# A chain of attention and two feed-forward blocks: stage 1 of batches 2 and 3 moved to slots 36 to 50, and splits tied to their slot

## The chip, the cores and the metric

The kernel runs on one core of a Trainium2 chip. The metric is the device time of one execution in microseconds; the time before is the median of three runs. A core has a matrix engine (PE, with its weight loads shown as PEld), a vector engine (DVE), an activation engine (ACT), a general engine (POOL) and a queue engine (SP) that only issues transfers here. Each engine works through its own list of instructions in order and waits where an input or a buffer isn't ready. Matrix products go to PSUM, which this kernel uses as eight banks.

## The reference

```python
def sm_attn(qq, kk, vv):                      # scale = 1/sqrt(64)
    s = scale * np.matmul(qq, kk.transpose(0, 1, 3, 2))
    s = s - np.max(s, axis=-1, keepdims=True)
    a = np.exp(s)
    a = a / (np.sum(a, axis=-1, keepdims=True) + 1e-09)
    return np.matmul(a, vv)
p_packed = sm_attn(p, k, v)                   # 32 rows per head: "stage 1", a pack
out = sm_attn(q, p_packed, p_packed)          # "stage 2", a spread
x = out.transpose(0, 2, 1, 3).reshape(4608, 512)
h = x @ w_in                                  # 512 -> 2048
x2 = (h / (1 + np.exp(-h))) @ w_out           # 2048 -> 512
y = ((x2 @ w1) * (x2 @ w2)) @ w3 @ wo2        # 512 -> 1024 -> 1024 -> 512
```

There are 8 batches, 8 heads, 576 positions, 64 values per head. All is float32. The weights arrive as 64-bit words and are turned into float32 on the chip ("decoding").

## The kernel before

**Numbers.** A float32 factor is split into a high part, in the type fp32r, and the rest as a low part; a product is three matmuls (`mm3`, lines 97 to 100): high × high, low × high, high × low. So nearly every factor has a split: `split_hi` (line 82) copies on ACT, `split_lo` (line 91) subtracts on DVE or, where the engine is given as G, on POOL.

**Slots.** The first feed-forward block is a list of 256 items (b, f, m): batch, half of its positions (288), and one of 16 slices of 128 of the 2048 inner columns. An item is a slot of the main loop. Batches 0 and 1 come first, with slices 0 to 7 in slots 0 to 31 and 8 to 15 in slots 32 to 63; batch 2 takes slots 64 to 95, and so on. A slot issues six matmuls into `ps_h`; sg (ACT, a tanh) and gg (DVE) from it, the split of gg into gh and gl (ACT and POOL), and twelve matmuls into `ps_x` for the item three slots back. The `ps_h` factors are a2, the result of stage 2 for this batch, and mq, a slice of the attention-packed w_in. `fetch` loads mq slices one by one through `mr` and splits them (DVE and POOL); it holds eight of them.

**What feeds the slots.** The product of softmax weights, packed values and w_in is regrouped: stage 1 (`Pack`) makes 32 packed rows per head; `PackIn` multiplies them, placed in the block matrix mbd, by w_in and stores the result in DRAM (`m_d`); stage 2 (`Spread`) turns q and the packed rows into softmax weights a2. A batch has two units of Pack and two of Spread (four heads each). For batch 2 the first slot that needs a2 is 64; `fetch` begins to load its `m_d` at slot 57. PackIn has 16 products: a w_in tile wz from DRAM, split into wi (three buffers), one mm3 into the bank `ps_m`, a copy ms (two buffers) and two stores.

**Order.** Each stream of side work is a Python generator. `over(lo, hi, units)` and `pack_in(lo, hi, batches)` spread a list's steps evenly over slots lo to hi (`due`), and the main loop advances the streams after each slot's own instructions. `chain` runs the units in a row: the steps of one unit also carry hooks, which load and split the next unit's inputs (`load`, `load_v`, `turn0`, `turn1`, `prepare`, `split_v0`). Packs and spreads share single buffers for the splits (x, v, e, pb), and packs, spreads and PackIn's products take turns on the two PSUM banks of the pool `ps_f`. A program written out by hand (`START`) orders the decoding of w_in and w_out (the "fill") through slot 34, beside the attention of batches 0 and 1.

This emission order is a priority, not the order on the engines. A planner with a timing model goes through the program: whenever an engine is free in the model, it takes the ready instruction that was emitted first. So later work may be pulled forward where an engine is idle, and late work falls behind its slot. `tc.issue_after(i)` forbids it for what stands in its block: on i's engine nothing of it goes ahead of i. `hold("sg", "gg")` does this with the last sg (on ACT) and the last gg (on DVE). Loads emitted in slots 0 to 15 are kept behind the last weight load; later ones are free (the lines `if i == KM` in the main loop and `move`).

Of the kernel before, what the change touches and what calls it, by code (L numbers as in the profile page):

```python
# [23 lines left out]
def attention_swiglu_chain(  # L24
# [54 lines left out]
    V, A, T, G, DMA = nc.vector, nc.scalar, nc.tensor, nc.gpsimd, nc.sync  # L79

    def act_copy(dst, src, mul=1.0):
        A.activation(out=dst, in_=src, func=ACTF.Copy, scale=mul)  # L82

    def split_hi(hi, src, on_vector=False):
        if on_vector:
            V.tensor_copy(out=hi, in_=src)  # L86
        else:
            act_copy(hi, src)

    def split_lo(lo, src, hi, eng=None):  # L90
        (eng or V).tensor_tensor(out=lo, in0=src, in1=hi.bitcast(F32), op=ALU.subtract)  # L91

    def split(hi, lo, src, on_vector=False, eng=None):
        split_hi(hi, src, on_vector)
        split_lo(lo, src, hi, eng)
# [8 lines left out]
    def hold(*names):  # L104

        stack = ExitStack()
        for x in names:
            stack.enter_context(tc.issue_after(behind[x]))
        return stack

    def move(out, in_, eng=DMA):

        out, in_ = (x.bitcast(F32) if x.dtype == F32R else x for x in (out, in_))
        with tc.issue_after(behind[eng]) if eng in behind else ExitStack():
            return eng.dma_start(out=out, in_=in_)  # L115
# [113 lines left out]
    def q_blocks(i, plain):  # L229
        return blocks(f"sbd{i}", [128, 2, 2, 128], plain)  # L230
# [4 lines left out]
    def small(n, name):  # L235
        return at.tile([128, n], F32, tag=f"{name}{n}", name=name, bufs=2)
# [7 lines left out]
    def work(shape, name):  # L244
        return at.tile(shape, F32, tag="work", name=name, bufs=3)

    def fill_blocks(dst, src, plain):

        quads = [slice(32 * h, 32 * h + 32) for h in range(4)]
        for r in quads:  # L250
            (act_copy if plain else V.tensor_copy)(dst[r, 0, :, r], src[r])  # L251
        for r in () if plain else quads:
            V.tensor_tensor(
                out=dst[r, 1, :, r], in0=src[r], in1=dst[r, 0, :, r].bitcast(F32), op=ALU.subtract
            )
# [44 lines left out]
    class Rows:  # L300
# [25 lines left out]
        def turn(self, f):  # L326

            if f not in self.halves or self.lane.plain:
                return
            if f == self.halves[0]:  # L330
                self.xp = self.lane.parts([128, 2, S], "x")
            x = [t[:, :, f * HS:(f + 1) * HS] for t in self.xp]
            split(*x, self.rows[f])
            self.x[f] = [[t[:, e] for t in x] for e in range(2)]

        def turn0(self):
# [18 lines left out]
            pass  # L355

        prepare = load_v = split_v0 = tail = nothing

    class Pack(Rows):

# [4 lines left out]
        N = 4  # L365
        PARTS = [(128, slice(0, 3)), (96, slice(3, 5))]
        HOOKS = {0: ["load_v"], 1: ["turn0"], 2: ["turn1", "prepare"], 3: ["split_v0"]}
# [14 lines left out]
        def prepare(self):  # L382
            if not self.lane.plain:
                self.pb = self.lane.parts([128, 2, 128], "pb")
                split(*self.pb, self.p)

        v_in_pieces = False

# [15 lines left out]
        def split_v(self, f):  # L404
            if self.lane.plain:
                return
            if f == 0:
                self.vp = self.lane.parts([128, 5, 4, 64], "v")
            r, cs = self.PARTS[f]
            hi, lo, src = (x[0:r, cs] for x in (*self.vp, self.v))  # L410
            split_hi(hi, src)
            split_lo(lo, src, hi, G)

        def split_v0(self):
            self.vp = [self.v]
# [2 lines left out]
        def steps(self):  # L418
            b, hg = self.b, self.hg
            sc = self.scores(self.pb)  # L420
            mx, nb, sm, rs = small(2, "mx"), small(1, "nb"), small(2, "sm"), small(1, "rs")
            for f in range(2):
                V.tensor_reduce(out=mx[:, f:f + 1], in_=sc[f][:, 0:HS], axis=AX.X, op=ALU.max)
            V.tensor_tensor(out=nb, in0=mx[:, 0:1], in1=mx[:, 1:2], op=ALU.max)
            V.tensor_scalar(out=nb, in0=nb, scalar1=-scale, scalar2=None, op0=ALU.mult)
            e1 = work([128, S], "e1")
            for f in range(2):
                A.activation(
                    out=e1[:, f * HS:(f + 1) * HS], in_=sc[f][:, 0:HS], func=ACTF.Exp, scale=scale,
                    bias=nb, accum_out=sm[:, f:f + 1],  # L430
                )
            self.split_v(1)
            yield
            ep = self.lane.parts([128, 5, 128], "e")
            pts = []
            o = 0
            for r, cs in self.PARTS:
                pt = self.lane.bank("ps_t")
                n = cs.stop - cs.start
                for j in range(n):  # L440
                    T.transpose(pt[0:r, 128 * j:128 * j + 128], e1[:, o:o + r], ident)
                    o += r
                pts.append(pt[0:r, 0:128 * n].rearrange("p (j n) -> p j n", j=n))
            for et, (r, cs) in zip(pts, self.PARTS):
                split_hi(ep[0][0:r, cs], et)
                if not self.lane.plain:
                    split_lo(ep[1][0:r, cs], et, ep[0][0:r, cs])
            V.tensor_tensor(out=rs, in0=sm[:, 0:1], in1=sm[:, 1:2], op=ALU.add)
            V.tensor_scalar(out=rs, in0=rs, scalar1=EPS, scalar2=None, op0=ALU.add)
            V.reciprocal(out=rs, in_=rs)  # L450
            yield
            po = self.lane.bank("ps_o")
            for c in range(5):
                r = 128 if c < 3 else 96
                self.lane.mm(
                    po[:, 0:256].rearrange("p (h d) -> p h d", h=4),
                    [x[0:r, c] for x in ep], [(x[c] if self.v_in_pieces else x[:, c])[0:r] for x in self.vp], c == 0, c == 4,
                )
                if c == 2:
                    yield  # L460
            self.pk = at.tile([128, 2, 64], F32, tag="pk", name="pk", bufs=2)
            for h in range(4):
                r = slice(32 * h, 32 * h + 32)
                A.activation(
                    out=self.pk[r], in_=po[r, 64 * h:64 * h + 64].unsqueeze(1).to_broadcast([32, 2, 64]),
                    func=ACTF.Copy, scale=rs[r],
                )
            pkT = at.tile([128, 2, 32], F32, tag="pkT", name="pkT", bufs=2)
            V.transpose(out=pkT, in_=self.pk[:, 0].rearrange("p (e i) -> p e i", e=2))
            fill_blocks(q_blocks(2 * (b % 2) + hg, self.lane.plain), pkT, self.lane.plain)  # L470
            yield
# [25 lines left out]
    class PackIn:  # L497


        N = 17  # L500
        HOOKS = {}
# [8 lines left out]
        turn0 = turn1 = prepare = load_v = split_v0 = tail = load  # L510

        def load_w(self, i):
            if i < 4 * CD:
                g, c = divmod(i, CD)
                z = at.tile([128, 512], F32, tag="z", name="wz", bufs=NZ)
                move(out=z, in_=wi_d[g, 128 * c:128 * c + 128])
                t = at.tile([128, 2, 512], F32R, tag="wi", name="wi", bufs=WI)
                split_hi(t[:, 0], z)
                split_lo(t[:, 1], z, t[:, 0], G)
                self.w[i] = t  # L520

        def steps(self):
# [27 lines left out]
    class Spread(Rows):  # L550


        N = 4
        HOOKS = {0: ["load_v"], 2: ["turn0"], 3: ["turn1", "prepare", "split_v0"]}
# [179 lines left out]
    def plain(us):  # L734
        for u in us:
            u.lane = lanes[0]
        return us
# [310 lines left out]
    def over(lo, hi, us):  # L1048
        units.extend(us)
        paces["x"].append((lo, hi, sum(u.N for u in us)))  # L1050

    def pack_in(lo, hi, bs):
        ins.append(PackIn(bs))
        paces["y"].append((lo, hi, PackIn.N))

    over(5, 14, plain([Spread(1, 0), Spread(1, 1)]))
    over(26, 38, [Pack(2, 0, 0), Pack(2, 1, 0), Pack(3, 0, 1), Pack(3, 1, 1)])
    pack_in(44, 66, [2, 3])
    over(44, 62, [Spread(2, 0), Spread(2, 1)])
    for b in range(2, B - 2, 2):  # L1060
        n, at0 = b + 2, b * H2
        over(at0 + 8, at0 + 29, [
# [338 lines left out]
```

## Time and profile before

| | |
|---|---|
| median of three runs | 1439.48 us (1436.52 to 1439.56) |
| profiled execution | 1437.96 us, its span 1436.1 us |
| PE busy in the span | 1390.7 us (97%) |
| DVE, ACT, POOL busy | 901.6, 672.2, 605.5 us |
| mean granted TensorE clock | 0.992 |

Slots 0 to 255 run from 44.7 to about 860 us; the second feed-forward block follows. The granted clock is a share of full speed, 2.4 GHz. "Busy" of PE counts a matmul until its end, and matmuls overlap, so the spacing of their starts tells more than their length.

### The profile page before, as it was taken

Reading aid. Unit: us, or ns where it says so; the run is one execution under the profiler, and the core shown is the slowest. Engines: PE = TensorE matmul, PEld = TensorE weight load, DVE = VectorE, ACT = ScalarE, POOL = GpSimd, SP = SyncE. Lnnn points to the kernel's source line nnn. Section 1 sums busy time; section 2 is a strip of 40 time slices with the busy share of each in tenths; the row PEclk is TensorE's granted clock in tenths of the full one; section 3 lists DMA queues with packets and bytes.
Section 4 is the critical chain, followed back from the end, with each engine's and each line's share of the span. In section 5 each row is a group of like instructions: output and inputs, shape, how many; then the busy total and the mean of one; then the engine's idle time right before and its main releaser. Section 6 shows DMA issues by size and latency. Waiting matters only on the chain.

```text
span 1436.1 us, 25890 instructions
## 1 busy us (share of the span) xinstructions
PE 1390.7 (97%) x9548; PEld 1308.4 (91%) x9548; DVE 901.6 (63%) x1687; ACT 672.2 (47%) x1474; POOL 605.5 (42%) x626
## 2 busy tenths in 40 slices
PE   7799899999999999999999999999999999999998
PEld 5578899899999999999998998999999999999998
DVE  5897756558766488666578855635454553645453
ACT  6866556655666555664556544323232231322221
POOL 2778755856779657687567534100000000000000
PEclk9999899999999999999999999999999999999999
DMA  8697544844568343563557667011010110101000
GB/s 319 198 308 253 163 150 142 265 152 146 170 184 249 123 155 121 170 190 116 178 162 252 204 228 298 23 38 46 15 60 1 60 29 31 59 2 60 1 30 30
DMA packets 135967, 193.07 MB, mean 134 GB/s; under 512 B 14496, under 2 KB 92576, under 8 KB 135328
## 3 DMA queue, kind: packets, MB, share of 16 engines
q1 hardware_dynamic: 125344, 178.82, 39.1%
q10 hardware_dynamic: 10496, 12.59, 2.5%
q8 instruction: 75, 1.23, 0.4%
q14 instruction: 52, 0.43, 0.1%
HBM read 132.38 MB, written 58.98 MB: 133 GB/s over the span
## 4 chain that ended last, share of the span: by engine, by line
PE 70%; DVE 9%; DMA 7%; issue 4%; POOL 4%; ACT 4%; SPq 2%; ACTq 0%; DVEq 0%; POOLq 0%
PE ps_ab L1236 24%; PE ps_x L100 6%; PE ps_x L98 6%; PE ps_x L99 6%; PE ps_o L98 5%; PE ps_o L99 5%; PE ps_o L100 5%; PE ps_h L98 3%; PE ps_h L100 3%; PE ps_h L99 3%; SPq L115 2%; DMA mr<-m_d 1%; DMA m_d<-ms 1%; POOL z L189 1%; DVE sbd L251 1%
## 5 line engine op out<-in xcount | busy, mean ns | idle before, releaser
L98 PE MATMUL ps_x<-gh,wo 128*128 128x288 f32 x1024 | 301.9, 298 | 2.7 <-ACT gh L82 1.2
L99 PE MATMUL ps_x<-gh,wo 128*128 128x288 f32 x1024 | 301.0, 296 | 0.0
L100 PE MATMUL ps_x<-gl,wo 128*128 128x288 f32 x1024 | 289.1, 297 | 1.9 <-POOL gl L91 1.6
L91 POOL TENSOR_TENSOR gl<-gg,gh 128x288 fp32r<-128x288 f32 x256 | 227.9, 893 | 101.5 <-ACT gh L82 82.5
L1236 PE MATMUL ps_ab<-xct,w 128*128 128x256 f32 x1728 | 223.0, 284 | 1.7 <-DVE r L1257 1.4
L1236 PEld LDWEIGHTS ps_ab<-xct,w 128*128 128x128 f32 x1728 | 215.6, 190 | 3.0 <-DVE r L1257 1.6
L98 PEld LDWEIGHTS ps_x<-gh,wo 128*128 128x128 f32 x1024 | 193.0, 189 | 6.1 <-DVE xs L883 2.0
L99 PEld LDWEIGHTS ps_x<-gh,wo 128*128 128x128 f32 x1024 | 193.2, 189 | 2.1 <-issue 1.2
L100 PEld LDWEIGHTS ps_x<-gl,wo 128*128 128x128 f32 x1024 | 188.1, 189 | 4.3 <-POOL gl L91 3.6
L82 ACT ACTIVATE gh<-gg 128x288 fp32r<-128x288 f32 x256 | 112.8, 443 | 165.8 <-DVE gg L846 158.2
L91 POOL TENSOR_TENSOR mq<-mr,mq 128x256 fp32r<-128x256 f32 x168 | 136.7, 814 | 109.0 <-DVE mq L86 54.4
L846 DVE SCALAR_TENSOR_TENSOR gg<-sg,ps_h 128x288 f32<-128x288 f32 x256 | 114.6, 448 | 107.3 <-ACT sg L841 55.3
L1236 PE MATMUL ps_ab<-xcb,w 128*128 128x256 f32 x1296 | 177.5, 283 | 0.7 <-ACT w L82 0.4
L98 PE MATMUL ps_h<-a,mq 128*128 128x288 f32 x512 | 155.9, 305 | 18.0 <-DVE gg L846 13.8
L1236 PEld LDWEIGHTS ps_ab<-xcb,w 128*128 128x128 f32 x1296 | 168.1, 189 | 5.6 <-ACT w L82 0.6
L1257 DVE TENSOR_TENSOR r<-p,ps_ab 128x512 f32<-128x512 f32 x72 | 49.2, 683 | 184.3 <-PE ps_ab L1236 184.1
L99 PE MATMUL ps_h<-a,mq 128*128 128x288 f32 x512 | 152.4, 298 | 0.0
L100 PE MATMUL ps_h<-a,mq 128*128 128x288 f32 x512 | 151.9, 297 | 0.0
L841 ACT ACTIVATE sg<-ps_h 128x288 f32<-128x288 f32 x256 | 103.4, 404 | 82.3 <-PE ps_h L100 48.6
L98 PEld LDWEIGHTS ps_h<-a,mq 128*128 128x128 f32 x512 | 96.7, 189 | 25.9 <-DVE gg L846 19.0
L82 ACT ACTIVATE p<-ps_ab 128x512 f32<-128x512 f32 x72 | 43.1, 598 | 146.2 <-PE ps_ab L1236 139.8
L100 PE MATMUL ps_o<-w,abh 128*128 128x512 f32 x280 | 109.5, 391 | 0.0
(172 smaller groups left out, 2645.3 us busy)
## 6 DMA issues: line engine op xcount, KB each, us to landing
mr<-m_d SPq DMA_DIRECT2D x144, 128.0 KB, 2.6
raw<-in_moe_w_dram SPq DMA_DIRECT2D x32, 512.0 KB, 4.4
wz<-wi_d SPq DMA_DIRECT2D x48, 256.0 KB, 3.8
m_d<-ms SPq DMA_DIRECT2D x96, 128.0 KB, 3.0
x_d<-xs SPq DMA_DIRECT2D x20, 576.0 KB, 3.4
raw<-in_moe_w_out_dram SPq DMA_DIRECT2D x22, 512.0 KB, 4.3
out_dram<-ob SPq DMA_DIRECT2D x36, 256.0 KB, 2.0
vr<-in_v_dram SPq DMA_DIRECT2D x14, 640.0 KB, 4.1
```

The source lines that it names most:

```text
L82: A.activation(out=dst, in_=src, func=ACTF.Copy, scale=mul)
L91: (eng or V).tensor_tensor(out=lo, in0=src, in1=hi.bitcast(F32), op=ALU.subtract)
L98: T.matmul(out=dst, lhsT=wh, rhs=xh, start=start, stop=False)
L99: T.matmul(out=dst, lhsT=wl, rhs=xh, start=False, stop=False)
L100: return T.matmul(out=dst, lhsT=wh, rhs=xl, start=False, stop=stop)
L115: return eng.dma_start(out=out, in_=in_)
L189: G.tensor_tensor(out=z, in0=z, in1=word(I32, 0), op=ALU.add)
L251: (act_copy if plain else V.tensor_copy)(dst[r, 0, :, r], src[r])
L841: ins = A.activation(out=sg, in_=ps, func=ACTF.Tanh, scale=0.5)
L846: ins = V.scalar_tensor_tensor(out=gg, in0=sg, scalar=1.0, in1=ps, op0=ALU.add, op1=ALU.mult)
L1236: T.matmul(out=bank[:, x], lhsT=w[:, wp], rhs=xt[:, kt, xp], start=first and (x, kt, n) == (0, 0, 0), stop=last and (x, kt, n) == (1, 1, 2 ...
L1257: V.tensor_tensor(out=dst, in0=p, in1=q, op=op)
```

## The change

Stage 1 of batches 2 and 3 (four packs) is emitted over slots 36 to 50 instead of 26 to 38. A new unit, `Pause`, stands ahead of them at slots 33 to 36: it does nothing itself, but its hooks load and split the first pack's inputs there (before, the hooks of the last Spread of batch 1 did, at slots 10 to 13). Stage 2 of batch 2 goes from 44–62 to 50–63 and PackIn for batches 2 and 3 from 44–66 to 50–70. The splits of q, k, p, v (in all batches that use them) and of PackIn's w_in tiles are emitted inside a `hold`, so that they don't go ahead of the sg and gg of the slot in which they are emitted.

```diff
--- before.py
+++ after.py
@@ -330,7 +330,8 @@
             if f == self.halves[0]:
                 self.xp = self.lane.parts([128, 2, S], "x")
             x = [t[:, :, f * HS:(f + 1) * HS] for t in self.xp]
-            split(*x, self.rows[f])
+            with hold("sg", "gg"):
+                split(*x, self.rows[f])
             self.x[f] = [[t[:, e] for t in x] for e in range(2)]
 
         def turn0(self):
@@ -356,6 +357,17 @@
 
         prepare = load_v = split_v0 = tail = nothing
 
+    class Pause(Rows):
+
+
+        N = 2
+        HOOKS = {0: ["load_v", "turn0", "prepare"], 1: ["turn1", "split_v0"]}
+        load = turn0 = turn1 = Rows.nothing
+
+        def steps(self):
+            yield
+            yield
+
     class Pack(Rows):
 
 
@@ -382,7 +394,8 @@
         def prepare(self):
             if not self.lane.plain:
                 self.pb = self.lane.parts([128, 2, 128], "pb")
-                split(*self.pb, self.p)
+                with hold("sg", "gg"):
+                    split(*self.pb, self.p)
 
         v_in_pieces = False
 
@@ -408,8 +421,9 @@
                 self.vp = self.lane.parts([128, 5, 4, 64], "v")
             r, cs = self.PARTS[f]
             hi, lo, src = (x[0:r, cs] for x in (*self.vp, self.v))
-            split_hi(hi, src)
-            split_lo(lo, src, hi, G)
+            with hold("sg"):
+                split_hi(hi, src)
+                split_lo(lo, src, hi, G)
 
         def split_v0(self):
             self.vp = [self.v]
@@ -515,8 +529,9 @@
                 z = at.tile([128, 512], F32, tag="z", name="wz", bufs=NZ)
                 move(out=z, in_=wi_d[g, 128 * c:128 * c + 128])
                 t = at.tile([128, 2, 512], F32R, tag="wi", name="wi", bufs=WI)
-                split_hi(t[:, 0], z)
-                split_lo(t[:, 1], z, t[:, 0], G)
+                with hold("sg"):
+                    split_hi(t[:, 0], z)
+                    split_lo(t[:, 1], z, t[:, 0], G)
                 self.w[i] = t
 
         def steps(self):
@@ -1054,9 +1069,10 @@
         paces["y"].append((lo, hi, PackIn.N))
 
     over(5, 14, plain([Spread(1, 0), Spread(1, 1)]))
-    over(26, 38, [Pack(2, 0, 0), Pack(2, 1, 0), Pack(3, 0, 1), Pack(3, 1, 1)])
-    pack_in(44, 66, [2, 3])
-    over(44, 62, [Spread(2, 0), Spread(2, 1)])
+    over(33, 36, [Pause()])
+    over(36, 50, [Pack(2, 0, 0), Pack(2, 1, 0), Pack(3, 0, 1), Pack(3, 1, 1)])
+    pack_in(50, 70, [2, 3])
+    over(50, 63, [Spread(2, 0), Spread(2, 1)])
     for b in range(2, B - 2, 2):
         n, at0 = b + 2, b * H2
         over(at0 + 8, at0 + 29, [
```

## Rows read from the trace of the kernel before

**Rows 1.** Busy times by stretch (us, instructions): PE, PEld, DVE, ACT, POOL; clock; DMA

```profile
60.00:137.65 77.65, 70.97 (x451) 61.90 (x451) 65.30 (x98) 52.47 (x112) 64.32 (x60) 1.00 0.93 302
137.65:176.85 39.20, 33.11 (x208) 31.33 (x207) 31.83 (x57) 21.92 (x55) 33.32 (x32) 0.87 0.49 145
...
231.90:268.00 36.10, 36.10 (x249) 34.50 (x247) 26.95 (x52) 21.86 (x47) 23.83 (x24) 1.00 0.73 223
```

**Rows 2.** PE matmuls into ps_h by stretch: us, busy (x count), clock, DMA share, GB/s

```profile
0.00:137.60 137.60, 28.75 (x156) 0.98 0.84 277
...
137.65:176.85 39.20, 10.93 (x60) 0.87 0.49 145
...
189.90:231.90 42.00, 13.58 (x84) 1.00 0.44 139
459.75:471.65 11.90, 4.77 (x30) 1.00 0.70 203
```

**Rows 3.** PE's waits from 137.7 to 176.9: total us, times, longest

```profile
PE ps_h L98 <- DVE gg L846: 4.8, 4, 2.7
```

**Rows 4.** Two stretches with a lower granted clock, columns as in Rows 1

```profile
154.20:157.50 3.30, 3.30 (x15) 3.30 (x15) 2.03 (x5) 3.04 (x9) 3.30 (x4) 0.50 0.92 261
...
167.90:174.60 6.70, 6.05 (x25) 6.05 (x26) 5.00 (x15) 2.21 (x6) 3.11 (x5) 0.50 0.30 98
```

**Rows 5.** PE in order of time: start us, us, line, what it writes and reads

```profile
139.69 0.30 PE L98 MATMUL ps_s<-x,pb 128*128 128x288 f32 x1
...
164.01 0.27 PE L478 MATMUL ps_pk<-ident,pk 128*128 128x128 f32 x1
...
189.86 0.27 PE L478 MATMUL ps_pk<-ident,pk 128*128 128x128 f32 x1
...
231.95 0.27 PE L478 MATMUL ps_pk<-ident,pk 128*128 128x128 f32 x1
...
236.43 0.29 PE L100 MATMUL ps_s<-x,sbd 128*128 128x288 f32 x1
...
254.94 0.29 PE L100 MATMUL ps_s<-x,sbd 128*128 128x288 f32 x1
...
267.16 0.30 PE L98 MATMUL ps_h<-a,mq 128*128 128x288 f32 x1
...
295.23 0.30 PE L98 MATMUL ps_s<-x,pb 128*128 128x288 f32 x1
...
313.17 0.27 PE L478 MATMUL ps_pk<-ident,pk 128*128 128x128 f32 x1
```

**Rows 6.** DVE in order of time, with the idle time before and its releaser

```profile
246.93 0.76 DVE L91 TENSOR_TENSOR a<-sT,a 128x576 fp32r<-128x576 f32 x1
...
259.21 0.29 DVE L86 CAST mq<-mr 128x256 fp32r<-128x256 f32 x1 [1.49 <-DMA mr<-m_d]
...
266.98 0.97 DVE L91 TENSOR_TENSOR a<-sT,a 128x576 fp32r<-128x576 f32 x1 [0.42 <-ACT a L82]
```

**Rows 7.** Two load issues by time, and load sizes: count, KB, us to landing

```profile
73.20 2.62 SPq L115 DMA_DIRECT2D vr<-in_v_dram  x1
106.19 0.59 SPq L115 DMA_DIRECT2D pr<-in_p_dram  x1
...
vr<-in_v_dram SPq DMA_DIRECT2D x14, 640.0 KB, 4.1
...
kq<-in_k_dram SPq DMA_DIRECT2D x26, 288.0 KB, 3.6
```

**Rows 8.** The tile ms, 230 to 290 us: duration ns min/median/max, first and last start

```profile
L115 SPq DMA_DIRECT2D m_d<-ms x32: 445/570/1062, 239.4 to 284.8; - x32
L82 ACT ACTIVATE ms<-ps_m x16: 577/582/602, 238.3 to 283.2; 128x512 f32<-128x512 f32 x16
...
DMA to landing us min/median/max: 2.3/2.9/5.4
```

**Rows 9.** The tile wi, 140 to 235 us, columns as in Rows 8

```profile
L91 POOL TENSOR_TENSOR wi<-wz,wi x3: 1274/1343/1353, 153.9 to 160.0; 128x512 fp32r<-128x512 f32 x3
```

## Prediction

> **What bounds the kernel now.** The profiled execution took 1437.96 us: its span of 1436.1 and 1.9 around it. The median of the runs shown is 1439.48, 1.5 more; I work on the former and add 1.5 at the end.
>
> First the stretches [rows 1]. The reader should see three kinds. In 60 to 137.65 us the DMA engines are 0.93 busy at 302 GB/s, and PE idles for 6.7 of 77.65 us. In 137.65 to 176.85 PE is busy for 33.1 of 39.2 us at a granted clock of 0.87, while DVE (31.8) and POOL (33.3) are nearly as full. In 231.9 to 268 PE is busy throughout.
>
> Then the slots. Each issues six ps_h matmuls. 156 have started by 137.60 us, so slot 26 starts at about 137.7; the next 60, slots 26 to 35, take up to 176.85. A slot with nothing beside it takes 11.9 / 5 = 2.38 us [rows 2], so these ten should need 23.8 us and took 39.2. In the 15.4 us between lie the first pack's PE work and the scores of the second. A pack costs PE about 4.3 us (the 42.0 us between two pack ends hold 84 ps_h [rows 2], so 14 slots or 33.3 us, and two packs); the second's scores are 12 matmuls at 2.38 / 18 = 0.13 us, 1.6. That leaves 9.5 us of real loss. PE waited 4.8 us there for gg on DVE [rows 3], and in two stretches ran 3.3 and 6.05 busy us at a granted clock of 0.50 [rows 4], which is the 1.2 of its two levels (1.2 and 2.4 GHz); half of that is 4.7. The two account for the 9.5.
>
> Last the chain that ends at slot 64, the first use of a2, batch 2's second-stage result. A pack is a serial chain (scores, exp, transposes, values, its closing transpose ps_pk) over two PSUM banks. The closing transposes of packs 1, 2 and 4 stand at 164.01, 189.86 and 231.95 [rows 5]: 24.3 us after the first scores at 139.69 for the pack in the fill, 25.9 for the second, 21.05 each for the last two. So four packs that are emitted over slots 26 to 38 really ran until slot 53; the emission window is not what paces them. The last a2 split ended at 266.98 + 0.97 = 267.95 [rows 6], and slot 64 starts at 267.16 [rows 5]. There is no slack.
>
> **The change, part by part.**
>
> *Packs 26–38 become 36–50, prepared by the Pause in 33–36.* Gain: slots 26 to 35 keep only the fill. I cost them at 23.8 plus 1.5 of rest (bounds 0.5 and 4, the fill's own waits). Before slot 26 pack 1's loads go: a vr of 640 KB and two kq of 288, 1.2 MB or 4.0 us at 302 GB/s, in the stretch where DMA is full [rows 1, 7]. But a load emitted from slot 16 on carries no hold, and the second pack's pr, emitted at slot 26, went out at 106.19, twelve slots ahead [rows 7]; so the new loads may be pulled forward as well. I take 3 us of 0 to 4.0, in which the splits of v, x and pb are counted that no longer stand before slot 26. Slot 36 then starts at 137.7 − 3 + 25.3 = 160.0 (155 to 165.5) instead of 176.9.
>
> The cost follows from the chain. Pack 1 starts at 160.0 instead of 139.7. In a stretch without the fill a first pack takes 313.17 − 295.23 = 17.9 us [rows 5]. The other three take 21.05 each, 63.2, since the same chain paces them and PE is full of slots; the last ps_pk stands at 160.0 + 17.9 + 63.2 = 241.1, against 231.95. By then 81.1 − 4 × 4.3 = 64 us have gone to slots, 27 of them: PE has just finished slot 62, and what is left needs a2.
>
> *Spread(2) and Pack-in from 50.* From the last ps_pk to a2 it took 36.0 us, in two pieces. First, up to the end of Spread(2,1)'s scores at 254.94 + 0.29 [rows 5]: 23.3 us, because the PSUM banks are handed out in emission order and six ps_m stood before those scores. Now five do (emitted in slots 51 to 55). With PE empty the two ms buffers pace them: a pair costs 0.58 on ACT, two issues of 0.57 and 2.9 to landing [rows 8], 4.6 us; the first ms starts about 4.5 after ps_pk, the fifth ends at 4.5 + 2 × 4.6 + 0.6 = 14.3 and the scores at 15.5. Upper bound: one ps_m less than now, 23.3 − 2.9 = 20.4. I take 17. Second, from those scores to a2: 12.7 us, with no PE work in it, so an idle PE doesn't shorten it; for Spread(2,0) it was 247.69 − 236.72 = 11.0 [rows 5, 6]. DVE waits in it for an mr load (1.49 us before the cast at 259.21). I take 12.7. So a2 is ready at 241.1 + 17 + 12.7 = 270.8 instead of 267.95, **2.9 us later**, though PE's own work would let slot 64 start at 267.2 − 9.5 − 3 = 254.7.
>
> In those 12.7 us the DVE split of a2 took 0.97 where the like one before took 0.76 [rows 6], with POOL busy for 23.8 of 36.1 us around it [rows 1]. The rule on the shared port (the Trainium skill, SBUF — State Buffer, Who interferes with whom) says that a DVE and a POOL instruction which both need it block each other wholly. By it the Spread would be quicker the fewer wi and mq splits run on POOL beside it; with the 11.0 in place of the 12.7 the sum would be 2.3 instead of 4.0. POOL's splits stay there, so I keep the row.
>
> The ps_m work is not lost: at 2.4 us each twelve fit into 29.7 us, eleven stand before slot 64 now. What remains is clock: PE is idle for about 15 us before slot 64, and the dips of [rows 4] lasted 3.3 and 6.7 us. Half of one dip of 3.3 is 1.7; part of it falls on idle time, or there are two: 1.5, bounds 0 and 4.
>
> *Holds.* A split is tied to the sg (on DVE the gg) of its emission slot. Where packs lag their window by up to 15 slots, that sg is long past and the hold is empty. It binds for the first pack (33 to 35) and for Pack-in's first three wi splits, which now run on POOL in 153.9 to 161.3, 1.34 us each, inside the fill though emitted at slot 44 [rows 9]; this gain is in the 9.5. For batches 4 to 7 I take −0.4 (−2 to +2): the PE loss there is small and has other causes.
>
> *Pack-in ends at 70 instead of 66.* fetch wants m_d's last group at slot 69, and it is emitted at 68; the mr loads then stand closer behind the stores on SP's queue, and DVE's mq casts, with gg behind them, wait for the loads. Cover: slot 76 is the first user. I take 0, up to +2, no gain since nothing gets earlier.
>
> Sum: 2.9 + 1.5 − 0.4 = +4.0. 1437.96 + 4.0 = 1442.0; against the median, 1443.5.
>
> **Rivals.**
> *The wait doesn't form (faster).* If slot 36 comes at 155.5 (the loads out of the full DMA stretch) and the tail takes 15.5 + 11.0, a2 is ready at 155.5 + 81.1 + 26.5 = 263.1, 4.9 earlier: about 1434. It decides at a2 before 265. For it: 302 GB/s before slot 26. Against: loads are pulled forward.
> *Gain and wait cancel (no change).* a2 within 2.9 us of today, about 1440. For it: the start is later by 20.3, the first pack quicker by 6.4, the second by 4.8, the tail by 6.3; one of them a little better is enough.
> *Nothing in the tail gets quicker (much slower).* If its 36.0 us stay, because DVE stands behind mr loads and POOL behind wi splits, a2 is at 277.1: +9.2, and 2 for the clock, about 1450.5. For it: the wait before 259.21. Against: PE no longer competes.
> *The holds do nothing*, since the queues lag: within 1 us of each case.
>
> **How the numbers follow.** 0.2% is 2.9 us, about what a measurement of this kernel can tell from no change. Forecast 0.32, much slower 0.10, cancel 0.28, faster 0.30; so slower 0.42, same 0.28, faster 0.30. The predicted time is the likeliest case's, 1443.5; its own range is 1441 to 1448. The range goes from 1430 (slot 36 at 155, short tail, holds worth 2, and 2 of rest) to 1452 (tail unshortened and slot 36 a little late).
>
> **What would show it.** Slot 36 at about 160, with no PE wait for gg over 1 us in 137 to 160; the first pack's scores in slot 36; the packs' ps_pk about 178, 199, 220 and 241; then PE idle, some 15 us in all, until a2's last split at about 271, with a granted clock below 1 near it. Wrong if packs follow each other in much less than seven slots, if slot 64 starts before 265, or if the time from slot 64 to the end changes by more than 2 us.

## The result, and the profile after

Slower: 1454.59 us median of four runs (1453.69 to 1460.12) against 1438.62 for the kernel before beside it, ratio 1.0121 (95% interval 1.0093 to 1.0149). The profiled execution took 1460.12 us, its span 1458.1: 22.0 more than before. A second set of runs of the same kernel (e13) gave 1456.47 and 1.0126 (1.0107 to 1.0145), with a span of 1452.7. The direction was as forecast; the size was not (4 us forecast, 16.0 measured, and 17.1 in e13), and the time lies outside the range.

Stretches of the kernel after by slot: 20 to 26 roughly, 26 to 36, 36 to 63, 63 to 66, 66 to 96. The columns are those of [rows 1].

```profile
120.00:144.10 24.10, 20.59 (x132) 19.17 (x132) 16.89 (x21) 16.78 (x37) 23.20 (x20) 0.93 0.82 278
144.10:166.10 22.00, 22.00 (x168) 22.00 (x167) 9.54 (x23) 11.43 (x28) 16.54 (x21) 1.00 0.42 120
166.10:252.10 86.00, 82.73 (x611) 82.24 (x610) 49.17 (x133) 44.37 (x113) 43.47 (x48) 0.96 0.43 138
252.10:293.90 41.80, 29.09 (x146) 22.56 (x146) 28.87 (x52) 22.19 (x43) 23.23 (x19) 0.92 0.54 153
293.90:385.70 91.80, 88.20 (x656) 86.58 (x655) 65.31 (x146) 49.90 (x122) 58.86 (x66) 1.00 0.60 182
```

The second line answers to the second of [rows 1]: slots 26 to 36 now take 22.0 us at a clock of 1.00 with PE never idle, instead of 39.2 at 0.87. Slot 36 starts at 166.1 instead of 176.9. The fourth line is where it goes: PE is idle for 12.7 of 41.8 us, and slot 66 starts 19.8 us later than before (293.9 against 274.1).

The ps_h matmuls by stretch (six to a slot), as in [rows 2]; the last line is the wait at slot 64:

```profile
0.00:144.10 144.10, 31.39 (x156) 24.68 (x157) 11.41 (x26) 10.39 (x26) 0.95 0.78 266
144.10:166.10 22.00, 9.58 (x60) 8.50 (x61) 4.08 (x9) 4.08 (x10) 1.00 0.42 120
...
252.10:281.80 29.70, 0.94 (x6) 0.70 (x6) 0.45 (x1) 0.41 (x1) 0.94 0.42 116
```

One slot in 29.7 us. The chain behind it, from PE's list, which answers to [rows 5], with the first matmul of slot 64:

```profile
165.32 0.29 PE L98 MATMUL ps_s<-x,pb 128*128 128x288 f32 x1
...
187.51 0.27 PE L492 MATMUL ps_pk<-ident,pk 128*128 128x128 f32 x1
...
211.04 0.27 PE L492 MATMUL ps_pk<-ident,pk 128*128 128x128 f32 x1
...
239.87 0.27 PE L492 MATMUL ps_pk<-ident,pk 128*128 128x128 f32 x1
...
261.01 0.27 PE L492 MATMUL ps_pk<-ident,pk 128*128 128x128 f32 x1
...
281.93 0.40 PE L98 MATMUL ps_h<-a,mq 128*128 128x288 f32 x1 [0.73 <-DVE mq L86]
```

First scores to last ps_pk: 95.7 us, in packs of 22.2, 23.5, 28.8 and 21.1. The last a2 split, on VectorE (DVE), answers to [rows 6]: it ends at 291.66, 23.7 us later than before.

```profile
290.42 1.24 DVE L91 TENSOR_TENSOR a<-sT,a 128x576 fp32r<-128x576 f32 x1 [0.75 <-ACT a L82]
```

PE's waits from 252.1 to 294 (total, times, longest), and the two stretches of low clock in it and the one at 215.3, columns as in [rows 4]:

```profile
PE ps_m L98 <- ACT ms L82: 8.4, 5, 4.1
PE ps_s L98 <- DVE s L586: 1.8, 1, 1.8
...
```

```profile
215.30:222.10 6.80, 6.04 (x25) 6.04 (x26) 3.65 (x12) 1.24 (x4) 1.59 (x2) 0.50 0.58 173
273.30:276.70 3.40, 3.09 (x9) 2.45 (x9) 1.97 (x3) 2.22 (x4) 0.97 (x1) 0.50 0.66 143
287.00:290.40 3.40, 2.92 (x6) 1.82 (x6) 1.59 (x2) 2.11 (x5) 3.17 (x4) 0.50 0.80 214
```

With no slot to run, PE has only pack-in's products and the spread's scores, and waits in them for the two ms buffers. The granted clock falls to 0.50 (the 1.2 of its two levels, 1.2 and 2.4 GHz) in or right after such gaps.

The 28.8 us of the third pack have a cause of their own. VectorE and GpSimd (POOL) after the second pack, where the L251 and L253 lines are the block fills, eight small copies and subtractions that place the packed rows in the block matrix sbd:

```profile
209.74 2.81 DVE L251 CAST sbd<-pkT 32x64 fp32r<-32x64 f32 x4
212.58 2.94 DVE L253 TENSOR_TENSOR sbd<-pkT,sbd 32x64 fp32r<-32x64 f32 x4
215.55 0.82 DVE L894 SCALAR_TENSOR_TENSOR xs<-ps_x,xs 128x288 f32<-128x288 f32 x2
...
217.38 0.20 DVE L504 CAST mbd<-ps_pk 64x64 fp32r<-64x64 f32 x1
```

```profile
211.20 3.74 POOL L91 TENSOR_TENSOR wi<-wz,wi 128x512 fp32r<-128x512 f32 x3
```

Pack-in's first three w_in splits, at 154 to 161 before [rows 9], are now held to slot 50 and run on GpSimd from 211.2 to 214.9. The eight fills beside them take 5.7 us (singly 0.41, 0.19, 0.84, 1.28, then 1.22, 1.19, 0.22, 0.22). xs, and with it PE, waits behind them:

```profile
216.06 0.61 PE L98 MATMUL ps_x<-gh,wo 128*128 128x288 f32 x1 [3.17 <-DVE xs L894]
```

The second half of the third pack's scores comes at 222.31, 11.2 us after the first; after the fourth's first half it took 5.0.

### The profile page after: what moved, and what is told of

The parts are those of the page before. It is cut to its first block, busy times and chain, and to the rows that moved or that the text cites. A ratio compares the mean times of both kernels' runs of the same rounds, so it can differ in the third digit from the quotient of the medians.

```text
span 1458.1 us, 25892 instructions
## 1 busy us (share of the span) xinstructions
PE 1397.7 (96%) x9548; PEld 1311.8 (90%) x9548; DVE 907.3 (62%) x1687; ACT 673.8 (46%) x1474; POOL 615.1 (42%) x626
## 4 chain that ended last, share of the span: by engine, by line
PE 73%; DVE 10%; ACT 6%; DMA 5%; issue 3%; SPq 1%; POOL 1%; ACTq 0%; DVEq 0%; POOLq 0%
PE ps_ab L1252 23%; PE ps_x L98 7%; PE ps_x L100 6%; PE ps_x L99 6%; PE ps_o L98 5%; PE ps_o L99 5%; PE ps_o L100 5%; PE ps_h L98 3%; PE ps_h L100 3%; PE ps_h L99 3%; SPq L115 1%; DVE gg L861 1%; DMA z<-late_d 1%; DVE mq L86 1%; ACT pk L478 1%
## 5 line engine op out<-in xcount | busy, mean ns | idle before, releaser
L91 POOL TENSOR_TENSOR gl<-gg,gh 128x288 fp32r<-128x288 f32 x256 | 230.9, 903 | 106.6 <-ACT gh L82 86.2
L98 PE MATMUL ps_h<-a,mq 128*128 128x288 f32 x512 | 156.1, 305 | 18.0 <-DVE gg L861 12.9
L99 PE MATMUL ps_o<-w,abl 128*128 128x512 f32 x280 | 109.6, 392 | 0.0
```

The costliest lines, as they stand in the source:

```text
L98: T.matmul(out=dst, lhsT=wh, rhs=xh, start=start, stop=False)
L99: T.matmul(out=dst, lhsT=wl, rhs=xh, start=False, stop=False)
```

## The experiments

The theory going in: the packs start late and need over 21 us each, so a2 is late and slot 64 waits. The rivals: the holds cost the time (A), or the later windows of stage 2 and pack-in do (B).

All numbers of the kernels in one table. "Start" is the first pack's first scores; "packs" the time from there to the last ps_pk; "tail" from that to the end of the last a2 split of batch 2; all from the traces. The three "loss" columns are PE's, over slots 20 to 36, 36 to 63 and 63 to 66: of the time between the starts of consecutive matmuls, what exceeds the usual spacing of their form (0.131 to 0.132 us for 288 columns), summed. All columns but the last two come from one trace per kernel; the two of the changed kernel differ by 2.6 us in a2 and 1.3 in the packs. Slot 20 itself starts between 118.0 and 127.1 us, and what is lost before it is in no loss column.

```
kernel                    start  packs  tail    a2   loss 20-36 36-63 63-66   median  ratio to before (95%)
before                    139.7   92.3  36.0  268.0        13.7   1.6   0.9  1438.62
changed                   165.3   95.7  30.7  291.7         6.5   7.8  19.1  1454.59  1.0121 (1.0093 to 1.0149)
e13 changed again         164.9   94.3  29.9  289.1         6.6   6.6  18.3  1456.47  1.0126 (1.0107 to 1.0145)
e1  holds only            142.8   94.8  37.9  275.6        13.2   5.0   0.8  1448.67  1.0078 (1.0063 to 1.0093)
e2  windows only          140.0  105.5  37.1  282.7        14.5   1.5  10.6  1448.96  1.0075 (1.0057 to 1.0093)
e3  holds, late tail      142.9   93.9  36.0  272.9        13.5   3.9   1.0  1448.58  1.0074 (1.0057 to 1.0091)
e4  packs at 30           148.4   90.1  41.9  280.3         9.3   3.5  12.2  1448.05  1.0074 (1.0057 to 1.0091)
e5  no hold on w_in       166.0   89.9  29.9  285.8         6.2   2.3  18.5  1454.85  1.0107 (1.0090 to 1.0123)
e6  hold on w_in alone    142.8   89.4  36.4  268.6         8.2   3.8   0.6  1439.61  1.0001 (0.9992 to 1.0011)
e7  hold on q, k, p alone 144.1   91.3  36.3  271.7        12.3   1.8   1.4  1441.99  1.0022 (1.0012 to 1.0032)
e8  w_in on VectorE       163.7   90.3  30.0  284.0         5.3   2.7  19.5  1453.90  1.0097 (1.0082 to 1.0112)
e9  hold on v alone       143.2   93.5  38.2  274.9        16.3   4.3   1.8  1447.17  1.0061 (1.0046 to 1.0076)
e10 Pause at 30           162.8   94.5  29.6  286.8         4.0   6.6  18.1  1457.27  1.0129 (1.0114 to 1.0144)
e11 changed, two packs    165.3      -     -  246.7         6.8   1.8   0.1  1424.42  0.9897 (0.9883 to 0.9912)
e12 before, two packs     143.4      -     -  243.9        11.0   1.4   0.1  1425.23  0.9908 (0.9892 to 0.9925)
e14 no hold on v          169.4   93.0  31.3  293.7        10.0   5.4  20.0  1464.58  1.0181 (1.0164 to 1.0198)
e15 spread first          163.5   94.2  23.7  281.4         5.4   6.8  20.9  1460.47  1.0147 (1.0131 to 1.0164)
e16 packs at 30, no holds 146.2   89.7  25.8  261.7        10.0   1.9   1.8  1441.95  1.0021 (1.0009 to 1.0033)
```

**e1, the holds without the windows** (all four holds put into the kernel before).

> The kernel before with the holds alone (on the splits of q, k, p, v and on the w_in tiles), all windows as before: packs at 26 to 38, stage 2 at 44 to 62, pack-in at 44 to 66, no Pause. Theory (the late start of the four packs and their pace of 21 us or more set a2, and slot 64 waits for it): the packs start where they did, so a2 stands near 268 us, slot 64 near 267, and the time is 1436 to 1442. Rival A (the holds are what costs: splits kept behind a late sg or gg stand where other work needs the engine, in this stretch and in batches 4 to 7): 1446 to 1455, with the last a2 split of batch 2 after 275 or the slots after 96 losing more than 3 us.

Rival A, by its time and by a2, if only just (275.6); slots 96 to 255 take 2.9 us longer than before. The holds alone cost 0.78% in the old windows.

**e2, the windows without the holds.**

> The changed kernel without any hold: windows and Pause alone. Theory: slot 36 about 166, last ps_pk 255 to 261, a2 of batch 2 at 285 to 292, the time 1449 to 1457; the pack that had pack-in's three w_in splits beside its block fills (28.8 us) gets some 3 to 6 us shorter, since these splits run ahead. Rival A (holds): 1437 to 1443, and a2 before 273.

Neither. The time is 5.6 us below the changed kernel's, and the mechanism is another: without the hold the planner takes the first pack's splits and scores forward into the fill, at slot 25, about where they stood before the change (139.69).

```profile
140.03 0.30 PE L98 MATMUL ps_s<-x,pb 128*128 128x288 f32 x1
```

Its scores start at 140.03, the first two packs take 33.2 and 30.4 us beside the fill, and a2 is late all the same. So this window moves the packs only together with the hold. (This trace is of the fastest of its four runs, 1445.31.)

**e3, the late tail** (packs at 26 to 38, holds kept).

```diff
-    pack_in(44, 66, [2, 3])
-    over(44, 62, [Spread(2, 0), Spread(2, 1)])
+    pack_in(50, 70, [2, 3])
+    over(50, 63, [Spread(2, 0), Spread(2, 1)])
```

> Packs at 26 to 38 as before (no Pause), but stage 2 at 50 to 63 and pack-in at 50 to 70, with the holds. Theory: the tail follows the last ps_pk, which stands near 232 as before (slot 53 or 54), so its later window costs little: 1437 to 1444, a2 by 270. Rival B (the later and longer window of stage 2 and pack-in is what makes a2 late): 1447 to 1456.

The expectation did not reckon with what the holds cost by themselves. Beside e1, which differs from it by this edit alone, it is 0.1 us lower: the later windows of stage 2 and pack-in cost nothing with the packs in their old place. Rival B is out for that place; late windows and late packs were not taken apart.

**e4, the packs six slots earlier.**

```diff
-    over(33, 36, [Pause()])
-    over(36, 50, [Pack(2, 0, 0), Pack(2, 1, 0), Pack(3, 0, 1), Pack(3, 1, 1)])
+    over(27, 30, [Pause()])
+    over(30, 44, [Pack(2, 0, 0), Pack(2, 1, 0), Pack(3, 0, 1), Pack(3, 1, 1)])
```

(and stage 2 and pack-in in the old windows.)

> Pause at 27 to 30 and packs at 30 to 44, six slots earlier than in the changed kernel; stage 2 and pack-in in the old windows (44 to 62, 44 to 66), with the holds. Theory: every ps_pk comes earlier than in the changed kernel by about what the start does, some 12 to 16 us; the last at 243 to 250, a2 at 272 to 280, slot 64 waits for it by 5 to 12 us less than in the changed kernel: 1440 to 1448. Rival A or B (place of the packs doesn't matter): as the changed kernel, 1452 to 1457 by A, 1437 to 1440 by B.

The start is 17 us earlier, the last ps_pk 22.6 (238.4), but a2 only 11.4: the tail grew to 41.9 us. The likely reason, not isolated, is that PE is still full of slots when it begins. The loss at slots 63 to 66 falls from 19.1 to 12.2, as expected; the time is at the upper end.

**e5, no hold on w_in; e8, its splits on VectorE.** e5 takes the `with hold("sg")` off the two splits in `load_w`. e8 keeps it:

```diff
-                    split_lo(t[:, 1], z, t[:, 0], G)
+                    split_lo(t[:, 1], z, t[:, 0], V if self.bs[0] == 2 and i < WI else G)
```

> The changed kernel without the hold on pack-in's w_in splits; the holds on q, k, p and v stay. Theory (in the changed kernel the first three of these splits, held to slot 50, stand on GpSimd exactly beside the block fills on VectorE after the second pack, which then took 0.84, 1.28, 1.22 and 1.19 us instead of 0.19 to 0.22, and PE lost about 5 us there): the splits go back to 140 to 165 us, the fills after the second pack take 0.2 us each, the third pack 21 to 24 us instead of 28.8, the last ps_pk stands near 255, a2 of batch 2 near 286, and the time is 1447 to 1451. Rival (that collision is not on the path that sets a2): within 2 us of 1454.6.

> The changed kernel, all holds kept, but the subtraction of the first three w_in splits of batches 2 and 3 on VectorE in place of GpSimd. Theory (GpSimd's splits block VectorE's block fills where both run): the fills after the second pack take 0.2 us each, VectorE has three subtractions more there (0.5 to 0.8 us each), and the third pack takes 22 to 25 us instead of 28.8: 1448 to 1452. Rival (the fills are slow for another reason, such as ACT's three casts or VectorE's own queue): the fills stay above 0.8 us or the pack above 27 us, 1453 to 1458.

VectorE in e8, the same eight fills:

```profile
208.14 1.72 DVE L251 CAST sbd<-pkT 32x64 fp32r<-32x64 f32 x4
209.89 0.96 DVE L253 TENSOR_TENSOR sbd<-pkT,sbd 32x64 fp32r<-32x64 f32 x4
```

2.7 us instead of 5.7, the third pack 23.4 instead of 28.8, the low clock after it gone; the same in e5 with 23.1. That GpSimd's three splits caused it is shown, by two different edits. But the times are 1453.90 and 1454.85: a2 comes 3 to 8 us earlier than in the two traces of the changed kernel, and of this 0.1 to 0.3% reaches the end (1.0107 and 1.0097 against 1.0121 and 1.0126), at the edge of what the intervals can tell. The expected 1447 to 1452 was missed; by its time e5 is the rival's. The collision is a part of the size, not its cause.

**e6, e7, e9, each hold alone in the kernel before.**

> The kernel before with the hold on pack-in's w_in splits alone. Theory (the 11 us that all holds cost there come from the splits of q, k, p and v): the three splits leave 154 to 161 us and go to about slot 44, between packs; 1435 to 1440. Rival (these held w_in splits are most of the cost): 1444 to 1449.

> The kernel before with the hold on the splits of q, k and p alone (behind the slot's sg and gg). Theory: most of the cost of the holds, 1443 to 1449: in the fill the splits of the first pack's p and k are kept to slots 12 to 14, where the last spread's softmax and the weight decoding stand on VectorE (its split of p took 2.07 us there in the run with all holds), and slot 26 comes at 142 to 145 instead of 137.7. Rival (the holds on v or on w_in): within 2 us of 1437.2.

> The kernel before with the hold on the splits of v alone. If the costs of the holds add up (all 11.5 us, q, k and p 3.3, w_in 0 to 1), v is worth some 7 to 8: 1443 to 1448, with the first slots of the fill (16 to 26) later by 3 to 6 us. Rival: v alone costs nothing (1436 to 1440), and the holds cost together what none costs alone.

w_in 0.01%, q, k and p 0.22%, v 0.61%: together 0.84, beside 0.78 for all of them at once (e1). They add up, and the one on v is most. e7 came between its two ranges. In e9 the first pack's v, split at 82.56 to 83.9 before, is split in two pieces, at slots 12 and 27:

```profile
97.64 0.85 ACT L82 ACTIVATE v<-vr 128x768 fp32r<-128x768 f32 x1
...
148.34 0.63 ACT L82 ACTIVATE v<-vr 96x512 fp32r<-96x512 f32 x1
```

So its single buffer vr is loaded anew at 158.1 instead of 111.7, and PE waits for gg at 105 to 110 for 3.4 us and between 160 and 180 for 6.2 (2.7 before). How one leads to the other was not isolated.

**e10, an earlier Pause** (30 to 33 in place of 33 to 36).

> The changed kernel with the Pause at 30 to 33 in place of 33 to 36; everything else as changed. Theory (the first pack took 22.2 us instead of the 17.9 of a pack without the fill, since the splits of its k, p and v stood between its own steps in slots 33 to 37): its inputs are split before slot 36, it takes 17.5 to 20 us, a2 of batch 2 comes 2 to 5 us earlier (280 to 285) and the time is 1449 to 1453. Rival (the steps of a pack wait for PE's and VectorE's queues whatever its inputs do): the first pack stays at 21 us or more, 1453 to 1457.

The rival. The splits of the inputs begin in slots 30 and 31, but for one piece of v, the scores start 2 us earlier and run in one go, and still the first pack takes 22.2 us. The same holds for all eight traces with the packs at 36 (e2, where they start in the fill, aside): the first pack takes 22.2 us and the second 23.5 in each, whatever the holds, the Pause or the number of packs. So the moment at which the inputs are split doesn't set the length of a pack here. That its own steps set it, each waiting its turn in PE's and VectorE's lists, is read from the trace and was not isolated: in the trace of the changed kernel the third pack's transposes follow its last exp after 2.1 us, its values the last split of e after 2.3, and the first mbd copy its ps_pk after 2.5.

**e11 and e12, stage 1 of batch 3 left out**, of the changed kernel and of the kernel before.

```diff
-    over(36, 50, [Pack(2, 0, 0), Pack(2, 1, 0), Pack(3, 0, 1), Pack(3, 1, 1)])
+    over(36, 43, [Pack(2, 0, 0), Pack(2, 1, 0)])
```

> The changed kernel without stage 1 of batch 3 (its two packs are left out, so batch 3 is computed from other data): packs of batch 2 at 36 to 43, all else as changed. Theory (slot 64 waits for a chain of four packs and the tail): the chain is two packs, 45 us, shorter; a2 of batch 2 stands before 250, PE's loss at slots 63 to 66 falls from 19 us to under 3, and with two packs of PE work (8.6 us) less the time is 1424 to 1432. Rival (another thing paces slots 63 to 66, such as the slices of w_in through DRAM): loss over 8 us there, 1436 to 1447.

> The kernel before without stage 1 of batch 3 (left out as in the run beside it), packs of batch 2 at 26 to 32: the base for that run. Theory: nothing waits for a2 before either, so only the work goes, 8.6 us: 1427 to 1432. The run beside it should then be lower than this one by what the fill gains from the later packs (6 to 9 us in PE's losses over slots 20 to 36), less what the holds cost (3 to 11): from 5 us lower to 3 us higher. Rival (the later start gives the fill nothing): 4 us or more higher.

Slots 63 to 66 in e11 (the columns of [rows 1]):

```profile
250.70:259.20 8.50, 8.50 (x62) 8.24 (x61) 4.91 (x8) 4.98 (x13) 8.27 (x9) 1.00 0.74 208
```

PE is never idle, and a2 is complete at 246.7:

```profile
245.90 0.76 DVE L91 TENSOR_TENSOR a<-sT,a 128x576 fp32r<-128x576 f32 x1 [0.76 <-ACT a L82]
```

With the chain two packs shorter the wait at slot 64 is gone, and the rest of the change comes out even: 1424.42 against 1425.23. By the ratios the two packs cost 2.24% in the new place (1.0121 − 0.9897) and 0.92% in the old (1 − 0.9908); the difference, 1.32%, is as large as the whole slowdown (1.21 to 1.26%). (The collision is in it: in e11 the block fills run before the splits begin.) The fill does gain: the loss over slots 20 to 36 is 4.2 us less in e11 than in e12. e12 is lower than expected: leaving out two packs saves the kernel before 12.9 us, more than their 8.6 us of PE work.

**e13, the changed kernel again.**

> The changed kernel once more, unaltered. The first profile of it was the longest of its four runs (1460.12 against 1453.7 to 1454.9). If the block fills beside the held w_in splits are part of the program's order, they stand there again (fills of 1.2 us near 211, third pack 27 to 29 us) in a run of 1453 to 1458; if they were chance, the third pack takes 22 to 24 us.

The collision is part of its order: VectorE's fills and GpSimd's splits stand as in the first profile.

```profile
209.28 2.80 DVE L251 CAST sbd<-pkT 32x64 fp32r<-32x64 f32 x4
212.12 2.94 DVE L253 TENSOR_TENSOR sbd<-pkT,sbd 32x64 fp32r<-32x64 f32 x4
```

**e14, the changed kernel without the hold on v.**

> The changed kernel without the hold on the splits of v; all else as changed. Rival C (the hold on v, worth 9 us in the old windows, costs as much in the new ones): 1444 to 1448. Theory (in the old windows it costs by keeping the first pack's v to slot 12 and so its loads and splits back into the fill; with the Pause this split stands at slot 34 anyway, and what sets the time is the start of the packs): 1451 to 1456, a2 of batch 2 within 4 us of 288.

Both missed: 8 us more than e13 beside it, not less. The first pack's v goes back into the fill (split at 138.5), PE waits 2.7 us for gg after 140 (in the changed kernel not at all), and slot 36 comes at 170.2 instead of 165.7. A further 4 us is lost over slots 66 to 96, for a reason that stays open. The hold on v costs 9 us in the old windows and saves 8 to 10 in the new ones.

**e15, stage 2 ahead of pack-in.**

```diff
-    pack_in(50, 70, [2, 3])
-    over(50, 63, [Spread(2, 0), Spread(2, 1)])
+    pack_in(57, 70, [2, 3])
+    over(50, 58, [Spread(2, 0), Spread(2, 1)])
```

> The changed kernel with stage 2 of batch 2 at 50 to 58 and pack-in at 57 to 70, so that pack-in's products no longer stand before the spread's scores. Theory (of the 30 us from the last ps_pk to a2, the products between take some 8): a2 comes 20 to 25 us after the last ps_pk, 4 to 9 us earlier than in the changed kernel, while the first slices of w_in come later; the time is 1449 to 1453. Rival (then the slices of w_in, which need four products, a store and a load, are what slot 64 waits for): 1453 to 1459, with PE's waits at slot 64 on mq instead of a.

The rival, by its mechanism; the time is still above its range. The tail is 23.7 us, but now the products of pack-in come after the scores: the first at 271.9 (264.7 in the changed kernel). So the first slice of w_in comes late. VectorE's next instruction after the last a2 split waits 5.2 us for its load:

```profile
286.60 0.29 DVE L86 CAST mq<-mr 128x256 fp32r<-128x256 f32 x1 [5.19 <-DMA mr<-m_d]
```

Slot 64 starts at 287.5, 6.1 us after a2 is there. Also the held w_in splits moved with the window, to slot 58, onto the fills after the third pack:

```profile
230.85 4.16 DVE L251 CAST sbd<-pkT 32x64 fp32r<-32x64 f32 x4
...
```

and the fourth pack takes 25.4 us.

**e16, packs at 30 to 44 without holds, stage 2 at 44 to 54, pack-in at 52 to 66.**

> A version that may be better than both: no holds at all, Pause at 27 to 30, packs at 30 to 44, stage 2 at 44 to 54 and pack-in at 52 to 66. Theory (start of the packs some 15 us earlier than in the changed kernel, the 5 us of the holds gone, 4 to 8 us of the tail gone): PE's loss at slots 63 to 66 falls to 0 to 7 us and the time is 1436 to 1444. Rival (without holds the planner pulls the first pack into the fill, so that the fill gains nothing and the chain is as long, as in the run with the windows alone): 1445 to 1450.

Within the theory's range: a2 at 261.7, 6 us earlier than before, and hardly a loss at slot 64. It is 13 to 15 us better than the changed kernel and 0.21% (0.09 to 0.33) worse than the kernel before. None of these versions that does all the work is faster than the kernel before.

## Why the prediction was wrong

**Slot 36 at 160.0: measured 166.1 (164.3 to 166.8 over the kernels with this start, 170.2 without the hold on v).** The half on slots 26 to 36 was right and even cautious: 22.0 us against 25.3. Of the difference 2.4 us is work that the sum counted there and that ran later: the stretch has 102 of the ten slots' 120 ps_x matmuls, as before (103). The other half had the wrong sign. The loads of the first pack leave their old place, but are pulled forward, from slot 33 to slots 21 to 23, among the loads of w_out:

```profile
126.05 1.05 SPq L207 DMA_DIRECT2D raw<-in_moe_w_out_dram  x2
127.15 0.43 SPq L115 DMA_DIRECT2D pr<-in_p_dram  x1
127.67 1.25 SPq L115 DMA_DIRECT2D kq<-in_k_dram  x2
128.97 0.59 SPq L115 DMA_DIRECT2D vr<-in_v_dram  x1
129.66 0.38 SPq L207 DMA_DIRECT2D raw<-in_moe_w_out_dram  x1
```

PE waits for gg there (3.5 us in 120 to 144), the clock is at 0.50 from 136.8 for 3.4 us, and slot 26 starts at 144.1 instead of the 134.7 of the sum. The prediction named the risk and took 3 of 4.0 us as gain. In e10, where they go at 113 to 115, the loss over slots 20 to 26 is 2.8 us instead of 6.4, but e8, with the loads where the changed kernel has them, loses 3.8: that they cause the wait was not settled.

**Four packs in 81.1 us: measured 95.7 and 94.3. This is the step that failed.** The first pack was taken at 17.9 (a first pack without the fill) and took 22.2; the others at 21.05 and took 23.5, 28.8 and 21.1. The kernel before needed 92.3, and the prediction put 11 of these down to the fill. The 17.9 was the fastest pack of its trace: the eight of batches 4 to 7, all outside the fill though in windows of their own, took 17.9, 20.6, 24.2, 23.9, 31.5, 21.0, 24.3 and 22.5 us, 23.2 on average, and four of that length make 93. In the fifteen kernels here with four packs, with starts from 140 to 169, inside and outside the fill, they took 89 to 96 us in all but e2, where it was 105.5. Of the 14.6 us too much, the held w_in splits make some 5 (e5, e8: 90), which the prediction missed as well: it counted the move of them as a gain inside the fill and did not ask what they would stand beside.

**The tail in 29.7 us: measured 30.65 (29.6 to 31.3 in the kernels with the windows of the changed one where PE runs out of slots).** Right, with its reason: with PE full it is 36 to 44 (26 in e16, whose stage 2 stands earlier). Five ps_m stand before the last scores, as said; the scores end 17.0 us after the last ps_pk (17 taken), and a2 is complete 13.7 later (12.7 taken).

**a2 at 270.8: measured 291.66.** 5.3 us from the start of the scores, 14.6 from the packs, 0.95 from the tail. PE would have begun slot 64 at 254.7 by the sum; slot 63 started at 252.1. The wait is the one that was forecast, but it ends 20.9 us later. The rival that came nearest in time, 1450.5 with the tail unshortened, is out all the same: the tail did shorten. Not all of the 23.7 us reaches the end: before, slot 66 started 6.1 us after a2 was complete, now 2.2, so there was a slack of some 4 us where the prediction saw none. Slot 66 is 19.8 us late in the longer of the two traces, 17.2 in the other; from there to the end little changes (1164.2 and 1161.4 us against 1162.0).

**Clock +1.5: 3.0 in this trace.** The two dips at the wait hold 6.0 us of busy PE at half speed, so 3.0, within the bounds of 0 and 4; in e13's trace they hold 11.5 and make 5.7, outside them. It is an upper bound, since PE waits there anyway. The dip at 215.3, another 3.0, comes with the collision and was not forecast. In the fill one dip is left, worth 1.7 against 4.7 before.

**Holds −0.4, for batches 4 to 7: slots 96 to 255 take 1.5 and 1.9 us longer in the two traces.** The sign was wrong, the size within the bounds of −2 and +2. What it put at nothing is the time before: in the old windows the holds cost 11 us (e1), and in that trace 6.6 of it by slot 66. In the new ones they are worth what the packs' place makes them: without any the time is 5.6 us lower, but the packs start at 140 again (e2); without that on v it is 8 to 10 us worse (e14). The rival "the holds do nothing" is out.

**Pack-in to 70 at nothing: right** (e3).

In the prediction the rule of the Trainium skill on the shared port (SBUF — State Buffer, Who interferes with whom) was weighed for the a2 split alone. By that rule, a VectorE instruction that needs the port waits for the whole of a GpSimd instruction that has it; the trace agrees: each of the slow fills takes 1.19 to 1.28 us beside a split of 1.26 to 1.30. The place where it counted was a run of short instructions, not the long one.

## What to carry to other kernels

When a serial chain is moved later, take its length from the whole chain as it ran before, not from its fastest links: a chain whose steps wait their turn in other lists does not shorten when its neighbour goes. Add start, length and tail, compare with the first use, and spend the slack only if there is any; here there were some 4 us. Tying work to a place is not free either: ask what stands at that place on the engines that share a resource, and test each tie in the new setting, since its sign can turn.

## What was not expected of the hardware

Of two instructions that collide, only VectorE's showed it: a block fill of 0.19 to 0.22 us took 1.19 to 1.28 beside GpSimd's 128x512 subtraction, about one fill to one subtraction. The subtractions took 1.26 to 1.30, and 1.27 to 1.35 where no fill stood beside them [rows 9]. With these splits gone from there (e5, e8) the slowest fill takes 0.83 and 0.84 us, beside a 128x288 subtraction of 0.81.
